# Running both layers' products as pairs of 64-row matmuls, with the order of issue taken from a list of operations

## The chip, the cores and the metric

One Trainium2 chip, one of its cores. The metric is device time in microseconds (us) of one execution, from three timed runs, and one further execution is recorded by the hardware profiler. Engines in the profile: PE is TensorE's matmul, PEld its weight load, DVE VectorE, ACT ScalarE, POOL GpSimd, SP SyncE, which here issues every DMA.

## What is computed

A softmax over 7 taps per position and head weighs a causal window of `x` (8192 positions of 192 features), and the result goes through two two-layer networks with 2048 hidden units each, one with a leaky ReLU, one with a squared ReLU. Weights are float64 and are split on the chip.

```python
w = softmax(weight_gen)                       # (2, 4096, 8 heads, 7 taps)
x = einsum('bshk,bskhg->bshg', w, window(x))  # 8192 x 192
h = x @ w_in;  x = maximum(0.01 * h, h) @ w_out         # 192 -> 2048 -> 192
h = x @ w_in2; r = maximum(h, 0); out = (r * r) @ w_out2
```

## The kernel before

Positions are worked on in 16 blocks of 512 (`tb`), hidden units in 16 chunks of 128 (`fc`). A phase is one network on one block, 16 steps; the phases run (0,0), (0,1), (1,0), (0,2), (1,1), (0,3) and so on, 32 in all, so 512 steps. Every float32 operand is held as a high and a low part in the type fp32r, and a product is high x high + low x high + high x low.

- `mm1` (L376) computes a chunk of hidden units: five matmuls with 128 x 128 weights on 512 columns. The 192 input features are 128 ("a") and 64 ("b"); the weights of the 64 lie twice in one tile, high in 64 rows and low in the other 64, and the moving tiles `bh`, `bl` hold the 64 features twice, so two matmuls cover them.
- `act_a` (L384, L385; L389, L390) applies the nonlinearity on ACT, `act_b` makes `gh` (L402, DVE, or ACT for the steps in `GH_SWAP`) and the low part `gl` (L404, DVE).
- `mm2` follows `LAG` = 3 steps behind. Network 0 (L417 to L421): five matmuls of 512 columns into `pa`, `pb`. Network 1 (L431, L434): the activations are the weights, `wo2` moves, four pairs of 384 and 192 columns into four banks `po`, whose rows are then positions, so the output needs no transposing.
- PSUM: two banks `ph`, two for `pa`, `pb`, four for `po`. Each network has accumulators of its own.
- `end1` turns the sums of network 0 into the input of network 1 with a DMA that swaps two halves (L446, L447); `end2` adds and stores.
- `conv_steps` is the windowed sum on DVE (softmax, 13 passes over 768 elements at L269 and L295), then a transposition: by PE for the first three blocks (`tr`), by DVE and a trip through DRAM for the others (`blocks`, `fr`).
- `Piece` turns 28 pieces of weights into high and low parts (ACT L138, L163; DVE L147 to L164); they are due in the first three phases.
- The order on each engine is the order of the main loop, with hand-set slots for the windowed sums (`CONV_AT`) and the pieces (`DUE`). All waits follow from the tiles.

Of the kernel before, what the change touches and what calls it, by code (L numbers as in the profile page):

```python
# [19 lines left out]
ORDER = [['b0', 'a0', 'o0', 'a1', 'o3', 'o1', 'o2', 'b1', 'a2', 'a3', 'o4', 'o5', 'o6', 'o7'], ['a0', 'o1', 'b0', 'o0', 'b1', 'a2', 'a1', 'o3', 'o2', 'a3', 'o4', 'o5', 'o7', 'o6']]  # L20
DUE = [[-2, -1, 1, 2, 3, 4, 5, 6, 7, 8, 9, 11, 12, 13], [18, 20, 22, 24, 28, 29, 30, 33, 36, 38, 39, 40, 44, 45]]
ENGINES = [[1, 1, 0]] * 28
POOL_TAPS = [3, 3, 3]
CONV_AT = [[0, 1, 4, 5, 6, 6, 7, 7, 8, 8, 10, 11, 12, 14, 14], [0, 0, 1, 4, 8, 8, 10, 13, 17, 18, 25, 26, 26, 28, 30]]
SIDE_AT = [[0, 1, 3, 4, 5, 6, 7, 8, 9, 10, 12, 14], [0, 1, 3, 4, 10, 11, 15, 17, 19, 20, 21, 22]]
GL_POOL = []
GH_SWAP = [0, 12, 14, 16, 17, 18, 22, 26, 31, 32, 33, 34, 35, 39, 40, 41, 44, 45, 47]
# [3 lines left out]
def kernel(  # L31
# [13 lines left out]

    nc = tc.nc
# [5 lines left out]
    G = D // H  # L52
# [3 lines left out]
    TPP = NT // P  # L56
    PPB = S // TPP
# [3 lines left out]
    NTB = TPP // TB  # L61
    NFC = FF // P
    DA = P
    DB = D - P
    CH = 4
    NCH = TPP // CH
    WCH = 4
    SW = FF // WCH
    OC = 2
    PH3 = 0  # L70
    PTAPS = dict(enumerate(POOL_TAPS))
    side_t = {}
# [26 lines left out]
    wo1 = {
        "ah": const.tile([P, NFC, DA], F32R, name="wo1ah"),  # L100
        "al": const.tile([P, NFC, DA], F32R, name="wo1al"),
        "b": const.tile([P, NFC, 2 * DB], F32R, name="wo1b"),
    }
    wo2 = const.tile([P, NFC, 2 * D], F32R, name="wo2")
# [5 lines left out]


    class Piece:
        def __init__(self, kind, l, c):
            self.kind, self.l, self.c = kind, l, c

        def load(self):
            kind, l, c = self.kind, self.l, self.c
            self.raw = raw = st.tile([P, SW, 2], I32, name="raw", tag="raw", bufs=3)
            if kind == "o":
                self.n = OC * D  # L120
                src = (w_out1, w_out2)[l]
                nc.sync.dma_start(
                    out=raw[:, : self.n, :].rearrange("p (f e) w -> p f e w", f=OC),
                    in_=src[c * OC * P : (c + 1) * OC * P].rearrange("(f p) e w -> p f e w", p=P),
                )
                return
            self.n = SW
            src = (w_in1, w_in2)[l]
            if kind == "a":
                nc.sync.dma_start(out=raw, in_=src[0:DA, c * SW : (c + 1) * SW, :])  # L130
            else:
                for h in range(2):
                    o = (2 * c + h) * SW
                    nc.sync.dma_start(out=raw[h * DB : (h + 1) * DB], in_=src[DA:D, o : o + SW, :])

        def scale(self):
            self.u = st.tile([P, SW], F32, name="wu", tag="wu", bufs=3)[:, : self.n]
            nc.scalar.activation(self.u, self.raw[:, : self.n, 1].bitcast(F32), AF.Copy, scale=2.0**-112)  # L138

        def join(self):  # L140
            u, n = self.u, self.n
            self.f = a = st.tile([P, SW], F32, name="wa", tag="wa", bufs=3)[:, :n]
            ui, ai = u.bitcast(I32), a.bitcast(I32)
            lo = self.raw[:, :n, 0].bitcast(U32)

            def rest():
                nc.vector.scalar_tensor_tensor(u, lo, 2.0**-52, u, op0=ALU.mult, op1=ALU.mult)  # L147
                (nc.gpsimd, nc.vector)[self.feng].tensor_tensor(a, a, u, op=ALU.add)  # L148

            return [  # L150
                lambda: nc.vector.tensor_scalar(
                    ai, ui, 3, 0x7FFFFFF8, op0=ALU.logical_shift_left, op1=ALU.bitwise_and
                ),
                lambda: nc.vector.scalar_tensor_tensor(ai, ui, SIGN, ai, op0=ALU.bitwise_and, op1=ALU.bitwise_or),  # L154
                lambda: nc.vector.tensor_scalar(ui, ai, SIGN_EXP, None, op0=ALU.bitwise_and),  # L155
                rest,
            ]

        def split(self):
            kind, l, c, f = self.kind, self.l, self.c, self.f  # L160

            def halves(h, lo, v):
                (nc.scalar.copy, nc.vector.tensor_copy)[self.heng](h, v)  # L163
                (nc.gpsimd, nc.vector)[self.leng].tensor_tensor(lo, v, h.bitcast(F32), op=ALU.subtract)  # L164

            if kind == "a":
                cs = slice(c * SW, (c + 1) * SW)
                halves(wi[l]["ah"][:, cs], wi[l]["al"][:, cs], f)
            elif kind == "b":
                h, lo = self.u.bitcast(F32R), f.bitcast(F32R)  # L170
                halves(h, lo, f)
                for j in range(2):
                    o = (2 * c + j) * SW
                    js = slice(j * DB, (j + 1) * DB)
                    nc.sync.dma_start(out=wi[l]["b"][0:DB, o : o + SW].bitcast(F32), in_=h[js].bitcast(F32))
                    nc.sync.dma_start(out=wi[l]["b"][DB:P, o : o + SW].bitcast(F32), in_=lo[js].bitcast(F32))
            else:
                fs = slice(c * OC, (c + 1) * OC)
                r = f.rearrange("p (f e) -> p f e", f=OC)
                if l == 0:  # L180
                    halves(wo1["ah"][:, fs, :], wo1["al"][:, fs, :], r[:, :, 0:DA])
                    halves(wo1["b"][:, fs, 0:DB], wo1["b"][:, fs, DB : 2 * DB], r[:, :, DA:D])
                else:
                    halves(wo2[:, fs, 0:D], wo2[:, fs, D : 2 * D], r)


    pieces = [
        (d, Piece(k[0], l, int(k[1:]))) for l in range(2) for d, k in zip(DUE[l], ORDER[l])
    ]
    for q, (d, p) in enumerate(pieces):  # L190
        p.feng, p.leng, p.heng = ENGINES[q]
    due = dict(pieces)


    x_flat = x.rearrange("b (p t) d -> (b p) t d", t=TPP)
    wg_flat = weight_gen.rearrange("b (p t) h k -> (b p) t h k", t=TPP)
    out_flat = out.rearrange("(p t) d -> p t d", t=TPP)
    xc_t = {}
    wg_t = {}
    wn_t = {}  # L200

    def load_chunk(c):
        xc = xp.tile([P, HALO + CH, D], F32, name="xc", tag="xc")
        wg = xp.tile([P, CH, H, K], F32, name="wg", tag="wg")
        if c == 0:
            nc.sync.dma_start(out=wg, in_=wg_flat[:, 0:CH])
            nc.gpsimd.memset(xc[0:1, 0:HALO, :], 0.0)
            nc.gpsimd.memset(xc[PPB : PPB + 1, 0:HALO, :], 0.0)
            nc.sync.dma_start(out=xc[:, HALO : HALO + TB, :], in_=x_flat[:, 0:TB, :])
            for b in range(B):  # L210
                o = TPP - HALO
                nc.sync.dma_start(
                    out=xc[b * PPB + 1 : (b + 1) * PPB, 0:HALO, :],
                    in_=x[b, o : o + (PPB - 1) * TPP, :].rearrange("(p t) d -> p t d", t=TPP)[:, 0:HALO, :],
                )
        else:
            nc.sync.dma_start(out=wg, in_=wg_flat[:, c * CH : (c + 1) * CH])
            nc.sync.dma_start(out=xc[:, HALO:, :], in_=x_flat[:, c * CH : (c + 1) * CH, :])
            nc.sync.dma_start(out=xc[:, 0:HALO, :], in_=xc_t[c - 1][:, CH : CH + HALO, :])
# [386 lines left out]
```

## Time and profile before

| | us |
|---|---|
| median of three runs (1262.72 to 1264.82) | 1264.58 |
| the profiled execution | 1262.62 |
| its span in the trace | 1260.8 |
| PE busy | 1207.7 (96%) |
| PE weight loads busy | 1023.9 (81%) |
| DVE busy | 822.7 (65%) |
| ACT busy | 678.0 (54%) |

Matmuls are pipelined, and their busy times overlap: a 512-column matmul shows 0.39 to 0.41 us of busy time, while one starts every 0.23 us. So a rate is read from the distance of starts, not from busy times. The same holds in smaller measure for ACT and DVE. The span is divided, in the reading below, into the time up to the first product, the first three phases, the 29 phases after them, and the end.

### The profile page before, as it was taken

The numbers are of one execution on the slowest core, as the hardware profiler recorded it, in microseconds if no ns is written. First come the engines' busy times: TensorE is split into PE (matmuls) and PEld (weight loads), VectorE is DVE, ScalarE is ACT, GpSimd is POOL, SyncE is SP. The second block draws the span as 40 slices with busy tenths as digits, with TensorE's granted clock in tenths as the row PEclk, the third lists the DMA queues.
The fourth block names the chain that finished last, engine by engine and source line by source line (L and its number), as shares of the span: only waits on it lengthen the run. The fifth ranks groups of instructions, "written<-read, shape, count | busy, mean of one in ns | idle before, by whom it ended". The sixth has DMA issues, their size and how long they took to land.

```text
span 1260.8 us, 16315 instructions
## 1 busy us (share of the span) xinstructions
PE 1207.7 (96%) x5912; PEld 1023.9 (81%) x5912; DVE 822.7 (65%) x1413; ACT 678.0 (54%) x1246; POOL 2.8 (0%) x8
## 2 busy tenths in 40 slices
PE   1689899999999999999999999999999999999997
PEld 1467688988888898888888888888888889888896
DVE  7999975757566575756657575665757556573453
ACT  2555665555555464555546455554555555455553
POOL 0000000000000000000000000000000000000000
PEclk9899999999999999999999999999999999999999
DMA  6424310202011020200202010020201100010000
GB/s 196 117 89 116 108 46 8 66 13 74 13 26 60 1 74 13 69 17 10 72 5 73 13 59 28 9 67 11 74 13 56 30 10 30 13 38 13 9 14 13
DMA packets 41120, 55.70 MB, mean 44 GB/s; under 512 B 4178, under 2 KB 30290, under 8 KB 41040
## 3 DMA queue, kind: packets, MB, share of 16 engines
q1 hardware_dynamic: 41040, 54.66, 14.4%
q8 instruction: 46, 0.75, 0.2%
q14 instruction: 34, 0.28, 0.1%
HBM read 28.11 MB, written 11.40 MB: 31 GB/s over the span
## 4 chain that ended last, share of the span: by engine, by line
PE 89%; DVE 8%; issue 1%; ACT 1%; DMA 0%; SPq 0%; DVEq 0%
PE ph L376 45%; PE po L431 15%; PE po L434 7%; PE pa L417 4%; PE pb L419 4%; PE pa L421 4%; PE pb L420 4%; PE pa L418 4%; DVE tmp L269 1%; DVE gl L404 1%; DVE wu L147 1%; DVE wa L154 1%; DVE wa L148 1%; DVE att L295 1%; DVE wu L155 1%
## 5 line engine op out<-in xcount | busy, mean ns | idle before, releaser
L404 DVE TENSOR_TENSOR gl<-g,gh 128x512 fp32r<-128x512 f32 x512 | 353.5, 691 | 260.9 <-ACT gh L385 232.9
L431 PE MATMUL po<-wo,gh 128*128 128x384 f32 x1024 | 307.1, 355 | 0.0
L384 ACT ACTIVATE g<-ph 128x512 f32<-128x512 f32 x256 | 153.5, 600 | 248.0 <-PE ph L376 246.8
L389 ACT ACTIVATE g<-ph 128x512 f32<-128x512 f32 x256 | 153.1, 598 | 198.7 <-PE ph L376 198.7
L434 PE MATMUL po<-wo,gl 128*128 128x192 f32 x1024 | 257.4, 251 | 2.5 <-DVE gl L404 2.5
L434 PEld LDWEIGHTS po<-wo,gl 128*128 128x128 f32 x1024 | 195.7, 191 | 14.1 <-DVE gl L404 3.2
L431 PEld LDWEIGHTS po<-wo,gh 128*128 128x128 f32 x1024 | 193.0, 188 | 11.9
L390 ACT ACTIVATE g<-g 128x512 f32<-128x512 f32 x256 | 162.1, 633 | 8.1
L402 DVE CAST gh<-g 128x512 fp32r<-128x512 f32 x247 | 104.1, 422 | 79.2 <-ACT g L390 79.2
L385 ACT ACTIVATE gh<-ph 128x512 fp32r<-128x512 f32 x256 | 152.3, 595 | 0.0
L376 PE MATMUL ph<-xah,wi0ah 128*128 128x512 f32 x256 | 103.7, 405 | 8.1 <-ACT wi0ah L163 4.5
L376 PE MATMUL ph<-xah,wi0al 128*128 128x512 f32 x256 | 102.9, 402 | 3.5 <-DVE wi0al L164 3.5
L376 PE MATMUL ph<-xah,wi1ah 128*128 128x512 f32 x256 | 105.2, 411 | 0.3 <-ACT gh L385 0.3
L417 PE MATMUL pa<-gh,wo1ah 128*128 128x512 f32 x256 | 102.5, 400 | 2.7 <-ACT wo1ah L163 2.2
L418 PE MATMUL pa<-gh,wo1al 128*128 128x512 f32 x256 | 102.2, 399 | 2.4 <-DVE wo1al L164 2.4
L420 PE MATMUL pb<-gl,wo1b 128*128 128x512 f32 x256 | 102.2, 399 | 2.3 <-DVE gl L404 2.3
L376 PE MATMUL ph<-xbl,wi0b 128*128 128x512 f32 x256 | 102.8, 402 | 0.0
L419 PE MATMUL pb<-gh,wo1b 128*128 128x512 f32 x256 | 102.4, 400 | 0.0
L421 PE MATMUL pa<-gl,wo1ah 128*128 128x512 f32 x256 | 102.3, 400 | 0.0
L376 PE MATMUL ph<-xbl,wi1b 128*128 128x512 f32 x256 | 102.1, 399 | 0.0
L376 PE MATMUL ph<-xbh,wi0b 128*128 128x512 f32 x256 | 102.1, 399 | 0.0
L376 PE MATMUL ph<-xal,wi0ah 128*128 128x512 f32 x256 | 101.8, 398 | 0.0
(79 smaller groups left out, 1564.9 us busy)
## 6 DMA issues: line engine op xcount, KB each, us to landing
xc<-xc SPq DMA_DIRECT2D x15, 576.0 KB
xc<-in_x_dram SPq DMA_DIRECT2D x16, 384.0 KB
raw<-in_moe_w_out_dram SPq DMA_DIRECT2D x16, 384.0 KB
sc<-xb SPq DMA_DIRECT2D x13, 384.0 KB
out_dram<-ot SPq DMA_DIRECT2D x52, 96.0 KB
raw<-in_moe_w_in_dram SPq DMA_DIRECT2D x8, 512.0 KB
bw<-bs SPq DMA_DIRECT2D x32, 128.0 KB
xa<-sc SPq DMA_DIRECT2D x52, 64.0 KB
```

Of the source, the lines that this page charges most:

```text
L376: nc.tensor.matmul(ph, lhsT=w[a][:, fs], rhs=xs[b], start=(i == 0), stop=(i == len(terms) - 1))
L384: nc.scalar.activation(g, ph, AF.Prelu, alpha=0.01)
L389: nc.scalar.activation(g, ph, AF.Relu)
L390: nc.scalar.activation(g, g, AF.Square)
L404: eng.tensor_tensor(gl, g, gh.bitcast(F32), op=ALU.subtract)
L417: nc.tensor.matmul(pa, lhsT=wo1["ah"][:, fc, :], rhs=gh, start=first, stop=False)
L418: nc.tensor.matmul(pa, lhsT=wo1["al"][:, fc, :], rhs=gh, start=False, stop=False)
L419: nc.tensor.matmul(pb, lhsT=wo1["b"][:, fc, :], rhs=gh, start=first, stop=False)
L420: nc.tensor.matmul(pb, lhsT=wo1["b"][:, fc, :], rhs=gl, start=False, stop=last)
L421: nc.tensor.matmul(pa, lhsT=wo1["ah"][:, fc, :], rhs=gl, start=False, stop=last)
L431: nc.tensor.matmul(po, lhsT=gh[:, ts], rhs=wo2[:, fc, :], start=first, stop=False, skip_group_check=True)
L434: nc.tensor.matmul(po[:, 0:D], lhsT=gl[:, ts], rhs=wo2[:, fc, 0:D], start=False, stop=last, skip_group_check=True)
```

## The change

- **Products.** The array is used as two halves of 64 rows, `HALVES`. A step is a pair of chunks. In `mm1` each half computes one chunk of the pair from three 64-feature blocks: "a", "b" and a new moving tile "s", "a" with its halves exchanged. That is nine pairs of 64-row matmuls for two chunks. In `mm2`, for both networks, the two halves take the upper and lower 64 rows of the same chunk, into accumulators of their own: ten pairs of 512 columns for two chunks. All matmuls now have 512 columns.
- **PSUM.** Two tiles `ph` of two banks; four banks `q0` to `q3` that both networks' accumulators use in turn.
- **Activations** are 1024 wide; network 1 takes three ACT passes (`Relu`, `Square` twice) and no DVE copy. `LAG` is 2 pairs.
- **Ends.** `total` adds the two halves' sums (one ACT copy, one DVE addition). `end2` transposes by DVE in 32 x 32 blocks and stores rows of 32 elements; positions are assigned to partitions so that these land right.
- **Inputs.** Windows are loaded whole; "s" comes from two DMAs (`swap`), for the first two blocks from a third PE transposition. Weight pieces are 18 instead of 28.
- **Order.** Every operation is entered in a list with an engine, an estimated cost and a priority; `Plan.issue` goes through the list once and issues, engine by engine, what can start first. PE keeps strict priority order.

```diff
-        terms = [("ah", "ah"), ("al", "ah"), ("b", "bh"), ("b", "bl"), ("ah", "al")]
-        for i, (a, b) in enumerate(terms):
-            nc.tensor.matmul(ph, lhsT=w[a][:, fs], rhs=xs[b], start=(i == 0), stop=(i == len(terms) - 1))
+            terms = [(wh, "h", s) for s in (0, 1, 2)] + [(wl, "h", s) for s in (0, 1, 2)]
+            terms += [(wh, "l", s) for s in (0, 1, 2)]
+            for i, (w, hl, s) in enumerate(terms):
+
+                for d in range(2):
+                    c = s if d == 0 else (1, 0, 2)[s]
+                    nc.tensor.matmul(
+                        ph.t[:, d, :],
+                        lhsT=w[HALVES[d], c, j, :],
+                        rhs=xs["asb"[s] + hl].t[HALVES[d]],
+                        start=(i == 0),
+                        stop=(i == len(terms) - 1),
+                    )
...
+        if l == 0:
+            pl.op("ACT", W, pr, [ph], [gh], lambda: nc.scalar.activation(gh.t, ph.t, AF.Prelu, alpha=0.01))
+            pl.op("ACT", W, pr, [ph], [g], lambda: nc.scalar.activation(g.t, ph.t, AF.Prelu, alpha=0.01))
+        else:
+            pl.op("ACT", W, pr, [ph], [g], lambda: nc.scalar.activation(g.t, ph.t, AF.Relu))
+            pl.op("ACT", W, pr, [g], [gh], lambda: nc.scalar.activation(gh.t, g.t, AF.Square))
+            pl.op("ACT", W, pr, [g], [g], lambda: nc.scalar.activation(g.t, g.t, AF.Square))
+        pl.op(
+            "DVE", dve(2 * N), pr + 0.7, [g, gh], [gl],
+            lambda: nc.vector.tensor_tensor(gl.t, g.t, gh.t.bitcast(F32), op=ALU.subtract),
+        )
...
+        if first:
+            acc_t[l] = [
+                [pl.buf(ps, [P, N], F32, n, f"q{2 * d + i}", 1) for i, n in enumerate(("pa", "pb"))] for d in range(2)
             ]
...
+        def prods(terms, g, begin, end):
+            for i, (c, w) in enumerate(terms):
+                for d in range(2):
+                    wt = wo[l][HALVES[d], 2 * j + c, :]
+                    nc.tensor.matmul(
+                        acc[d][w == "b"].t,
+                        lhsT=wt[:, {"ah": slice(0, P), "b": slice(P, 2 * P), "al": slice(2 * P, 3 * P)}[w]],
+                        rhs=g.t[HALVES[d], c, :],
...
+        for n, (ks, g) in enumerate(((("ah", "al"), gh), (("b",), gh), (("ah",), gl), (("b",), gl))):
...
+    def total(acc, i, v, hold, pr):
+        o = pl.op("ACT", act(N), pr, [acc[1][i]], [v, *hold], lambda: nc.scalar.copy(v.t, acc[1][i].t))
+        pl.op(
+            "DVE", dve(N), pr, [acc[0][i], v], [v],
+            lambda: nc.vector.tensor_tensor(v.t, acc[0][i].t, v.t, op=ALU.add),
+        )
...
+    def end2(tb, acc, pr):
+        oa, ob, bw = wide("oa"), wide("ob"), wide("bw")
+        total(acc, 0, oa, [], pr)
+        total(acc, 1, ob, [bw], pr)
+        ta = pl.buf(sb, [P, N], F32, "ta", "c", 3)
+        pl.op("SP", 0.5, pr, [ob], [bw], lambda: nc.sync.dma_start(out=bw.t[0:Q], in_=ob.t[Q:P]), late=0.5)
+        pl.op("DVE", dve(N), pr + 1, [oa], [ta], lambda: nc.vector.transpose(ta.t, oa.t))
...
+            for c in range(n):
+                v = src.t[32 * c : 32 * c + 32].rearrange("a (u e) -> a u e", e=32)
+                nc.sync.dma_start(out=out_rows[:, tb, :, 32 * (c0 + c) : 32 * (c0 + c + 1)], in_=v)
...
+        pl.op("SP", 2.0, pr + 1, [ta], [], lambda: store(ta, 0, 4), late=2.0)
+        pl.op(
+            "DVE", dve(N), pr + 2, [ob, bw], [ob],
+            lambda: nc.vector.tensor_tensor(ob.t[0:Q], ob.t[0:Q], bw.t[0:Q], op=ALU.add),
+        )
+        pl.op("DVE", dve(N), pr + 2, [ob], [oa], lambda: nc.vector.transpose(oa.t[0:Q], ob.t[0:Q]))
+        pl.op("SP", 1.0, pr + 2, [oa], [], lambda: store(oa, 4, 2), late=1.0)
...
+        local_sum(0, 0)
+        weights("i", 0, (1, 1, 2, 2, 2))
+        weights("o", 0, (1, 1, 2, 2, 2))
+        weights("i", 1, (2,) * 4)
+        weights("o", 1, (2,) * 4)
...
+                if j == (LAG if tb else 0) and l == 0 and tb + 1 < NTB:
+                    local_sum(tb + 1, at[0, tb + 1] - (4 if tb else 1), gate=() if tb == 0 else (starts[0, tb - 1],))
+                o = mm1(l, tb, j, i)
+                if j == 0:
+                    starts[l, tb] = o
+                activate(l, tb, j, i + 0.5)
             if i >= LAG:
-                mm2(*steps[i - LAG])
...
+                mm2(*steps[i - LAG], i + 0.5)
+        pl.issue()
```

## Rows read from the trace of the kernel before

**Rows 1.** The page's head and its part 4, shares of the last chain.
```profile
span 1260.8 us, 16315 instructions
...
PE 89%; DVE 8%; issue 1%; ACT 1%; DMA 0%; SPq 0%; DVEq 0%
```

**Rows 2.** Busy time by stretch; columns named in the first row, counts in brackets.
```profile
core 0: us, PE busy (x) PEld busy (x) DVE busy (x) ACT busy (x) POOL busy (x), PEclk, DMA share, GB/s
0.00:27.40 27.40, 1.96 (x9) 1.59 (x9) 20.36 (x33) 5.86 (x11) 2.81 (x8) 1.00 0.64 182
27.40:86.30 58.90, 44.83 (x153) 33.05 (x154) 57.19 (x116) 30.21 (x67) 0.00 (x0) 0.88 0.43 130
86.30:127.30 41.00, 39.06 (x162) 29.30 (x160) 38.65 (x71) 24.73 (x48) 0.00 (x0) 1.00 0.37 96
127.30:173.60 46.30, 42.00 (x208) 35.89 (x208) 44.84 (x84) 32.98 (x62) 0.00 (x0) 0.93 0.29 91
173.60:247.80 74.20, 74.20 (x370) 63.35 (x369) 46.72 (x79) 40.55 (x75) 0.00 (x0) 1.00 0.12 37
...
173.60:1253.40 1079.80, 1079.80 (x5386) 924.03 (x5384) 660.86 (x1111) 583.78 (x1060) 0.00 (x0) 1.00 0.11 32
```

**Rows 3.** Instructions of L376 from 128 to 250 us: count, durations, first and last start.
```profile
L376 PE MATMUL ph<-xah,wi0ah x17: 393/394/413, 173.6 to 247.8; 128*128 128x512 f32 x17
```

**Rows 4.** PE in order of time (start us, us), one step of network 0.
```profile
561.07 0.39 PE L376 MATMUL ph<-xah,wi0ah 128*128 128x512 f32 x1
...
563.40 0.39 PE L376 MATMUL ph<-xah,wi0ah 128*128 128x512 f32 x1
```

**Rows 5.** PE in order of time, one step of network 1.
```profile
602.89 0.41 PE L376 MATMUL ph<-xah,wi1ah 128*128 128x512 f32 x1
...
604.07 0.34 PE L431 MATMUL po<-wo,gh 128*128 128x384 f32 x1
...
605.20 0.41 PE L376 MATMUL ph<-xah,wi1ah 128*128 128x512 f32 x1
```

**Rows 6.** Weight loads (PEld) in order of time, around two short matmuls.
```profile
602.23 0.19 PEld L431 LDWEIGHTS po<-wo,gh 128*128 128x128 f32 x1
602.34 0.19 PEld L434 LDWEIGHTS po<-wo,gl 128*128 128x128 f32 x1
```

**Rows 7.** Groups by line: busy us, mean ns, idle before and releaser.
```profile
L404 DVE TENSOR_TENSOR gl<-g,gh 128x512 fp32r<-128x512 f32 x512 | 353.5, 691 | 260.9 <-ACT gh L385 232.9 <-PE po L434 1.4 <-PE ph L376 0.9
L402 DVE CAST gh<-g 128x512 fp32r<-128x512 f32 x247 | 104.1, 422 | 79.2 <-ACT g L390 79.2
...
L148 DVE TENSOR_TENSOR wa<-wa,wu 128x384 f32<-128x384 f32 (+1 forms) x28 | 17.2, 615 | 1.0
```

**Rows 8.** The last chain from 27 to 60 us: start us, us it takes.
```profile
36.37 0.60 DVE gl L404
...
54.28 0.87 DVE att L269
```

**Rows 9.** ACT in order of time: two 512-wide passes in a row.
```profile
93.42 0.59 ACT L445 COPY bs<-pb 128x512 f32<-128x512 f32 x1 [2.12 <-PE pb L420]
93.90 0.59 ACT L448 CAST xah<-pa 128x512 fp32r<-128x512 f32 x1
```

**Rows 10.** All engines at the end, in order of time.
```profile
1252.64 1.18 ACT L459 COPY ot<-po 128x192 f32<-128x192 f32 x4 [2.44 <-PE po L434]
...
1252.99 1.22 DVE L460 TENSOR_TENSOR ot<-po,ot 128x192 f32<-128x192 f32 x4 [1.54 <-ACT ot L459]
1253.02 0.36 PE L431 MATMUL po<-wo,gh 128*128 128x384 f32 x1
1253.21 0.25 PE L434 MATMUL po<-wo,gl 128*128 128x192 f32 x1
1253.38 2.44 SPq L463 DMA_DIRECT2D out_dram<-ot  x4
```

**Rows 11.** Waits of SP's queue: total us, times, longest.
```profile
SPq L334 <- DMA sc<-xb: 27.0, 13, 2.8
```

More of the change, by code (lines that the diff above doesn't have):

```diff
@@ L26, with __init__ @@
-GL_POOL = []
-GH_SWAP = [0, 12, 14, 16, 17, 18, 22, 26, 31, 32, 33, 34, 35, 39, 40, 41, 44, 45, 47]
+class Buf:
+    def __init__(self, make=None, ring=None):
+        self.make, self.ring = make, ring
+        self.writers, self.readers = [], []
+        self.left = 0
+        self.end = 0.0
+        self.t = None
+class Op:
+    def __init__(self, eng, cost, fn, prio, deps, bufs, late):
+        self.eng, self.cost, self.fn, self.prio = eng, cost, fn, prio
+        self.deps, self.bufs, self.late = deps, bufs, late
+        self.end = None
@@ new lines, with __init__, buf, op @@
+class Plan:
+    def __init__(self):
+        self.ops = []
+        self.rings = {}
+    def buf(self, pool, shape, dtype, name, tag, bufs):
+        return Buf(lambda i: pool.tile(shape, dtype, name=name, tag=f"{tag}_{i}", bufs=1), (tag, bufs))
+    def op(self, eng, cost, prio, reads, writes, fn, after=(), late=0.0):
+        deps = set(after)
+        for b in reads:
+            deps.update(b.writers)
+        for b in writes:
+            deps.update(b.readers or b.writers)
+        o = Op(eng, cost, fn, prio, deps, [], late)
+        for b in dict.fromkeys([*reads, *writes]):
+            o.bufs.append(b)
+            b.left += 1
+        for b in reads:
+            b.readers.append(o)
+        for b in writes:
+            if b.readers:
+                b.writers, b.readers = [], []
+            b.writers.append(o)
+        self.ops.append(o)
+        return o
+    def issue(self, gap=0.07):
+        free = {}
+        wire = 0.0
+        queues = {}
+        for o in self.ops:
+            queues.setdefault(o.eng, []).append(o)
+        for q in queues.values():
+            q.sort(key=lambda o: o.prio)
+        order = {}
+        def start_of(o):
+            t = 0.0
+            for d in o.deps:
+                if d.end is None:
+                    return None
+                t = max(t, d.end + (gap if d.eng != o.eng else 0.0))
+            need = {}
+            for b in o.bufs:
+                if b.t is None and b.make:
+                    need[b.ring] = need.get(b.ring, 0) + 1
+            for (tag, n), k in need.items():
+                slots = self.rings.setdefault(tag, [None] * n)
+                ends = sorted(s.end + gap if s else 0.0 for s in slots if not (s and s.left))
+                if len(ends) < k:
+                    return None
+                t = max(t, ends[k - 1])
+            return t
+        left = len(self.ops)
+        while left:
+            best = None
+            for e, q in queues.items():
+                f = free.get(e, 0.0)
+                pick = None
+                for n, o in enumerate(q):
+                    if e == "PE" and n:
+                        break
+                    if n > 60:
+                        break
+                    s = start_of(o)
+                    if s is None:
+                        continue
+                    s = max(s, f)
+                    if pick is None or s < pick[0] - 0.15:
+                        pick = (s, n, o)
+                    if s <= f:
+                        break
+                if pick and (best is None or pick[0] < best[0]):
+                    best = (*pick, e)
+            if best is None:
+                raise RuntimeError("no operation can start: " + str([(e, q[0].prio) for e, q in queues.items() if q]))
+            s, n, o, e = best
+            queues[e].pop(n)
+            for b in o.bufs:
+                if b.t is None and b.make:
+                    slots = self.rings[b.ring[0]]
+                    i = min((s.end if s else -1.0, i) for i, s in enumerate(slots) if not (s and s.left))[1]
+                    slots[i] = b
+                    b.t = b.make(i)
+            o.fn()
+            free[e] = s + o.cost
+            if o.late:
+                wire = max(wire, s + o.cost) + o.late
+                o.end = wire + 2.0
+            else:
+                o.end = s + o.cost
+            o.at = s
+            for b in o.bufs:
+                b.left -= 1
+                b.end = max(b.end, o.end)
+            left -= 1
@@ L104 @@
[L104 to L124, printed above, removed]
-                )
[L126 to L152, printed above, removed]
-                ),
-                lambda: nc.vector.scalar_tensor_tensor(ai, ui, SIGN, ai, op0=ALU.bitwise_and, op1=ALU.bitwise_or),
-                lambda: nc.vector.tensor_scalar(ui, ai, SIGN_EXP, None, op0=ALU.bitwise_and),
-                rest,
-            ]
[L159 to L184, printed above, removed]
@@ L187 @@
[L187 to L219, printed above, removed]
-        xc_t[c], wg_t[c] = xc, wg
@@ L458, in end2 @@
[L458 to L469 removed]
+    NPR = NFC // 2
@@ new lines, with act, dve @@
+    Q = 64
+    HALVES = (slice(0, Q), slice(Q, P))
+    LAG = 2
+    EARLY = 2
+    R = TB * H
+    const = ctx.enter_context(tc.tile_pool(name="const", bufs=1))
+    sb = ctx.enter_context(tc.tile_pool(name="sb", bufs=2))
+    dram = ctx.enter_context(tc.tile_pool(name="dram", bufs=2, space=bass.MemoryType.DRAM))
+    ps = ctx.enter_context(tc.tile_pool(name="ps", bufs=2, space=bass.MemoryType.PSUM))
+    pl = Plan()
+    def act(n):
+        return 0.17 + n / 1200
+    def dve(n):
+        return (n + 151) / 960
@@ new lines, with x_set, swap, go @@
+    XS = ("ah", "al", "sh", "sl", "bh", "bl")
+    def x_set():
+        return {k: pl.buf(sb, [P, N], F32R, f"x{k}", f"x{k}", 3) for k in XS}
+    x1 = []
+    taken = []
+    def swap(xs, pr):
+        for k in "hl":
+            def go(k=k):
+                to, of = xs["s" + k].t, xs["a" + k].t
+                nc.sync.dma_start(out=to[0:Q].bitcast(F32), in_=of[Q:P].bitcast(F32))
+                nc.sync.dma_start(out=to[Q:P].bitcast(F32), in_=of[0:Q].bitcast(F32))
+            pl.op("SP", 1.0, pr, [xs["a" + k]], [xs["s" + k]], go, late=1.0)
@@ new lines, in mm2 @@
+    def mm2(l, tb, j, pr):
+        gh, gl = g_t.pop((l, tb, j))
+        first, last = j == 0, j == NPR - 1
+        if first:
+            acc_t[l] = [
+                [pl.buf(ps, [P, N], F32, n, f"q{2 * d + i}", 1) for i, n in enumerate(("pa", "pb"))] for d in range(2)
+            ]
+        acc = acc_t[l]
+        def prods(terms, g, begin, end):
+            for i, (c, w) in enumerate(terms):
+                for d in range(2):
+                    wt = wo[l][HALVES[d], 2 * j + c, :]
[3 more added lines that the diff above has]
+                        rhs=g.t[HALVES[d], c, :],
+                        start=begin and i == 0,
+                        stop=end and i == len(terms) - 1,
+                    )
+        w = wo_b[l][j]
+        for n, (ks, g) in enumerate(((("ah", "al"), gh), (("b",), gh), (("ah",), gl), (("b",), gl))):
+            terms = [(c, k) for c in range(2) for k in ks]
+            to = [a[ks[0] == "b"] for a in acc]
+            pl.op(
+                "PE", len(terms) * MM, pr + 0.01 * n, [g, w], to,
+                lambda terms=terms, g=g, n=n: prods(terms, g, first and n < 2, last and n >= 2),
+            )
+        if last:
+            (end1, end2)[l](tb, acc, pr - 1)
@@ new lines, in total, with wide, end1, other @@
+    def total(acc, i, v, hold, pr):
+        o = pl.op("ACT", act(N), pr, [acc[1][i]], [v, *hold], lambda: nc.scalar.copy(v.t, acc[1][i].t))
+        pl.op(
+            "DVE", dve(N), pr, [acc[0][i], v], [v],
+            lambda: nc.vector.tensor_tensor(v.t, acc[0][i].t, v.t, op=ALU.add),
+        )
+        return o
+    def wide(name):
+        return pl.buf(sb, [P, N], F32, name, "w", 4)
+    def end1(tb, acc, pr):
+        xs = x_set()
+        x2.append(xs)
+        sa, bs, bw = wide("sa"), wide("bs"), wide("bw")
+        taken.append(total(acc, 0, sa, [*xs.values()], pr))
+        total(acc, 1, bs, [bw], pr)
+        def other():
+            nc.sync.dma_start(out=bw.t[0:Q], in_=bs.t[Q:P])
+            nc.sync.dma_start(out=bw.t[Q:P], in_=bs.t[0:Q])
+        pl.op("SP", 1.0, pr, [bs], [bw], other, late=1.0)
+        ah, al, bh, bl = (xs[k] for k in ("ah", "al", "bh", "bl"))
+        pl.op("ACT", act(N), pr + 1, [sa], [ah], lambda: nc.scalar.copy(ah.t, sa.t))
+        pl.op(
+            "DVE", dve(N), pr + 1, [sa, ah], [al],
+            lambda: nc.vector.tensor_tensor(al.t, sa.t, ah.t.bitcast(F32), op=ALU.subtract),
+        )
+        swap(xs, pr + 1)
+        pl.op(
+            "DVE", dve(N), pr + 2, [bs, bw], [bs], lambda: nc.vector.tensor_tensor(bs.t, bs.t, bw.t, op=ALU.add)
+        )
+        pl.op("ACT", act(N), pr + 2, [bs], [bh], lambda: nc.scalar.copy(bh.t, bs.t))
+        pl.op(
+            "DVE", dve(N), pr + 2, [bs, bh], [bl],
+            lambda: nc.vector.tensor_tensor(bl.t, bs.t, bh.t.bitcast(F32), op=ALU.subtract),
+        )
@@ L474, with weights, begin @@
     phases.append((1, NTB - 1))
-    PH3 = 0
-    if PH3:
-        phases = [(0, 0), (0, 1), (0, 2), (1, 0), (1, 1)]
-        for tb in range(3, NTB):
-            phases += [(0, tb), (1, tb - 1)]
-        phases.append((1, NTB - 1))
-    def plan(fs, tb):
-        if tb < 2 + PH3:
-            at = CONV_AT[tb]
-        else:
-            at = [0, 2, 3, 4, 6, 8, 10, 12, 14, 15, NFC + 1]
-            at += [NFC + 7 - k for k in range(len(fs) - 15, 0, -1)]
-            at += [NFC + 7, NFC + 7, NFC + 12, NFC + 14]
-        return list(zip(at, fs))
-    GH = set(GH_SWAP)
-    POOL_GL = set(GL_POOL)
-    steps = [(l, tb, fc) for l, tb in phases for fc in range(NFC)]
-    todo = []
-    with tc.manual_schedule():
-        load_chunk(0)
-        warm = cv.tile([P, 1], F32, name="warm", tag="warm", bufs=1)
+    at = {ph: i * NPR for i, ph in enumerate(phases)}
+    steps = [(l, tb, j) for l, tb in phases for j in range(NPR)]
+    def weights(kind, l, sizes):
+        j = 0
+        for n in sizes:
+            piece(kind, l, j, n, at[l, 0] + j + (LAG if kind == "o" else 0))
+            j += n
+    warm = const.tile([P, 1], F32, name="warm")
+    def begin():
         nc.vector.memset(warm, 0.0)
@@ L503 @@
         make_identity(nc, ident)
-        first = [p for d, p in pieces[:3]]
-        for p in first:
-            p.load()
-        load_chunk(1)
-        todo = conv_steps(0)
-        for f in todo[:4]:
-            f()
-        todo = todo[4:]
-        for _ in range(2):
-            todo.pop(0)()
-        side = side_t[0]
-        while side:
-            side.pop(0)()
-        first[0].scale()
-        first[1].scale()
-        for p in first[:2]:
-            for f in p.join():
-                f()
-                if todo[3:]:
-                    todo.pop(0)()
-            p.split()
@@ L579 @@
+    Plan.last = pl
 _INS = ["x", "weight_gen", "moe_w_in", "moe_w_out", "moe2_w_in", "moe2_w_out"]
```

526 lines of the change are left out of this document (226 added, 300 removed).

## The prediction

> **What bounds the kernel now.** I read the shares of the last chain first, then the busy time by stretch, then the starts on PE inside one step, then what surrounds the end. PE carries 89% of the last chain and DVE 8% [rows 1]. The stretches say where each counts [rows 2]. From 173.6 us, where the first step of phase (0,2) starts [rows 3], to 1253.4, PE is busy for the whole stretch at full clock, while DVE and ACT are busy for 61% and 54% of it: 29 phases in which only PE's rate counts. From 27.4 to 173.6 it is the other way: DVE is busy for 57.19 + 38.65 + 44.84 = 140.7 of 146.2 us (96%) and PE waits for weights that DVE is splitting; the granted clock there falls to a mean of 0.88 and 0.93 in two stretches, where PE had waited. So a change of PE's work pays in the 29 late phases, and a change of DVE's work in the first three.
>
> PE's rate has to be taken from starts. A step of network 0 lasts 563.40 - 561.07 = 2.33 us for ten matmuls of 512 columns, 0.233 each [rows 4]. A step of network 1 lasts 2.31: 1.18 for `mm1` and 1.13 for its four pairs of 384 and 192 columns, 0.283 a pair [rows 5]. The mean of both is 2.32, and 464 x 2.32 = 1076.5, plus the three lagging `mm2` (3 x 1.13), makes the 1079.8 of the stretch. The term is closed.
>
> **PE, late phases.** Let t be the distance from one pair of 64-row matmuls to the next. A step of the new kernel, two chunks of one network, has 9 + 10 = 19 pairs, so 19t against 2 x 2.32 = 4.64 us now. In columns: `mm1` goes from 5 to 4.5 matmuls per chunk, `mm2` of network 0 stays at 5, and that of network 1 rises from 4 x 576/512 = 4.5 to 5. The sum is 19.0 against 19.5, a gain of only 2.6%; the rest comes from network 1's four short pairs, which cost 1.13 us where 2304 columns at 0.233 per 512 would cost 1.05. Everything hangs on t, and no row of before shows a 64-row matmul. The bounds:
> - Below: weight loads. Two loads that followed each other as closely as any I found start 0.11 us apart [rows 6], and a pair needs two; if they share one path, t is no less than about 0.216.
> - Above: if the halves don't run together, t = 2 x 0.233 = 0.466.
> - Between: four PE instructions (two loads, two matmuls) were put through in 0.283 us in the short pairs [rows 5]; a pair at 0.233 asks for them 18% faster than any row shows for long.
>
> I take 0.233. It is the nearest row: a 512-column matmul whose weights load behind its predecessor, with two loads fitting into it. The halves touch different rows and different PSUM banks, so I see nothing that they would share but the path of instructions and that of loads. Then 232 steps x 19 x 0.233 = 1027.1, against 1076.5: 49.4 saved.
>
> **Sharing the accumulators.** `mm2` of the next phase wants `q0` to `q3` one `mm1` after the last `mm2` of this one, 9 x 0.233 = 2.1 us, and the "a" sums are complete 2 x 0.233 before that. Let T be the end of the step's `mm1`. "a" is complete at T + 1.88, visible some 0.17 later (a matmul's 0.39 of busy time less its 0.233 [rows 4]). ACT is in 1024-wide passes: two 512-wide ones start 0.48 apart [rows 9], so at most 0.96 for 1024. Two passes end at T + 2.1, the copy takes 0.59 [rows 9], the addition 0.69 (L404's, the same shape [rows 7]): T + 3.4 if DVE is free, T + 4.5 if it has just begun a 1024-wide subtraction. PE wants the banks at T + 2 x 2.21 = T + 4.4. So the wait is hidden unless DVE's order is unlucky; behind the addition on DVE stand `gl` and the windowed sum, which have a step of slack. Bounds 0 and 1 us for each of 29 boundaries; I take 0.15: 4.4 us.
>
> **ACT and DVE, late phases.** Per two phases (70.8 us) ACT has 8 x 2 + 8 x 3 passes x 0.96 = 38.4 plus about 4 for copies and casts, 60%. DVE: a 512-wide subtraction occupies 0.60 and a 768-wide pass 0.87 of the chain [rows 8], so 1.05 ns an element and 0.06 fixed, 1.14 for 1024; 16 x 1.14 + 13 x 0.87 + about 11 for the rest = 41, 57% (now 46.7 of 74.2 [rows 2]). The casts of L402, 247 on DVE [rows 7], are gone and cost ACT what is in the sum. Neither becomes a bound; if one did, the cover is 30 us per two phases. More DMA (the swaps, 32-element stores) has a share of 0.12 to grow from [rows 2], and each lands a phase or more before its use: nothing.
>
> **The first three phases.** DVE sets the pace up to step 24, so its work is the term. Pieces go from 28 [rows 7] to 18: 59 instructions fewer at 0.06 is 3.5, the columns stay. `gl`: 48 x 0.60 and seven casts at about 0.36 (0.422 [rows 7] less the 0.06) against 24 x 1.14, 3.9 less. The third transposed tile adds 2 x 0.60, the ends one pass and slightly longer ones, 0.8. Net 5.4 less: (0,2) starts at 168.2. PE alone would be there at 27.4 + 24 x 4.43 = 134, so DVE still decides. The first product: a third PE transposition (about 2 us) against a smaller first piece; I leave it at 27.4. For the list's order against the hand-set one I keep 15 us either way.
>
> **The end.** Now from PE's last slot (1253.21 + 0.09) to the span's end: 7.5 us, of which 5.0 follow SP's last issue (1253.38 + 2.44) [rows 10]. After: result visible 0.17, second ACT copy 0.59, addition 0.69, a DMA hop, addition, transposition (0.69 each), two issues of 0.6 (2.44 / 4) and the same 5.0. The hop I take from a wait for a DMA of the kind, 27.0 / 13 = 2.1 [rows 11], and 0.5 to issue. Sum 11.6.
>
> **Sum.** 168.2 + 1027.1 + 4.7 (two lagging `mm2`) + 4.4 + 11.6 = 1216.0 of span. The profiled execution of before took 1262.62 for a span of 1260.8, 1.8 outside it: 1217.8. The median of the runs is 2.0 above that execution: 1219.8, say 1220, 3.5% faster. The margin of 44.6 us is 0.010 us on each of 232 x 19 = 4408 pairs, so the change turns slower at t = 0.243.
>
> **The rivals.**
> - *The path of instructions decides (the other side).* PE needs four instructions a pair instead of two per full matmul. At 0.283, the densest that lasts in the trace, 4408 x 0.050 = 220 more: 1440. From t = 0.243 on it is slower than before; at 0.258, halfway, 1330. For it: no row shows 58 ns an instruction for long. Against it: what makes the short pairs dear fits their loads as well [rows 6]. By the Trainium skill, "TensorE: Matmul & The Clock Gate", section "Wait — 56ns, not 53.3ns?", a sequencer without hardware decode spends about 62 ns per MATMUL; if a load cost it as much, four would make 0.248 and some 1286 us, an estimate from that page; no row here shows it.
> - *The halves overlap only in part.* If a half's load must follow its partner's matmul start and the next pair waits for the later half, a load slot of 0.11 is added to each pair: t = 0.34, 4408 x 0.107 = 472 and some 15 in the first phases: about 1705. For it: no row of before shows that a half can run ahead of the other. Against: that order alone delays one half by a slot once, not each time. The Trainium skill's page named above, section "Measured speedup vs the span model", has four row tiles at 3.07 times one; that share, 0.77, would make t = 0.303 and about 1528 us, an estimate from the page. Its page "TensorEngine Tiling (Array Packing)", section "Key Properties", has tiles load and multiply in parallel, which is what I forecast.
> - *The halves don't run together, so the change doesn't do what it says.* t = 0.466: 4408 x 0.233 = 1027 more, and the first phases then take 27.4 + 24 x 19 x 0.466 = 240 instead of 168: about 2320.
> - *Boundaries wait.* The list puts a third ACT pass, two casts and a 1024-wide subtraction ahead of copy and addition: 0.96 + 0.96 + 1.14 on T + 3.4 is T + 6.4, 2 us late, 29 x 1.85 = 54 more: 1274. It turns slower at 1.7 us each.
> - *Pairs go faster.* If the 0.020 over 512 / 2400 = 0.213 is a change of weights that one half hides for the other, t falls to the loads' 0.216: 75 less, 1145.
>
> **How the numbers follow.** Forecast 0.58, with t from 0.230 to 0.240, boundaries from 0 to 0.6 and the first phases 15 either way: 1190 to 1255. Instructions 0.18, of which 0.07 below 1290; partial overlap and none together 0.06; boundaries 0.10 (1225 to 1290), half of it faster; faster pairs 0.08. To hold eight in ten the range takes the forecast, the boundaries and the lower part of the instructions' case: 1185 to 1290. A measurement of this kernel tells about 0.2% from no change. Faster: 0.58 + 0.08 + 0.05 = 0.71; same 0.02; slower 0.27.
>
> **What would show it.** In a late phase: starts of pairs 0.233 apart with both halves starting close together (right), or starts of single matmuls that far apart (no overlap). First `mm2` of a phase waiting for DVE's addition: more than 0.3 us means the boundary is priced too low. The first product of (0,2) at 153 to 183. If DVE's share is over 90% in late phases, I have missed work.

## The result and the profile after

The changed kernel takes 1281.4 us (median of four executions, 1279.5 to 1283.7) against 1264.5: a ratio of 1.0138, 95% interval 1.0118 to 1.0157, so 1.4% slower, more than its interval leaves to noise. 1220 was forecast.

| span in the trace, us | before | forecast | after |
|---|---|---|---|
| to the first product | 27.4 | 27.4 | 39.3 |
| the first three phases | 146.2 | 140.8 | 185.9 |
| from (0,2) to PE's last slot | 1079.7 | 1036.2 | 1047.8 |
| the end | 7.5 | 11.6 | 8.9 |
| whole span | 1260.8 | 1216.0 | 1281.9 |

The gain in the late phases is there: 31.9 us. The first two rows lose 51.6.

The page's head, the busiest engines and the shares of the last chain (now 80% PE, 8% DMA, where DMA had 0% [rows 1]):

```profile
span 1281.9 us, 22668 instructions
PE 1172.7 (91%) x9752; PEld 936.2 (73%) x9752; DVE 741.9 (58%) x887; ACT 745.7 (58%) x826; POOL 0.7 (0%) x6
...
PE 80%; DVE 9%; DMA 8%; ACT 1%; issue 1%; SPq 1%; DVEq 0%; ACTq 0%
```

Busy time by stretch, to be set beside [rows 2]: the first three phases, (0,2) and (1,1), (0,3) and (1,2), then all from (0,3) to the end of the products.

```profile
core 0: us, PE busy (x) PEld busy (x) DVE busy (x) ACT busy (x) POOL busy (x), PEclk, DMA share, GB/s
39.30:225.20 185.90, 127.20 (x885) 99.47 (x887) 141.70 (x195) 86.99 (x105) 0.00 (x0) 0.83 0.39 97
225.20:304.90 79.70, 74.12 (x612) 59.19 (x610) 53.60 (x64) 45.90 (x51) 0.00 (x0) 0.96 0.28 74
304.90:376.30 71.40, 71.40 (x612) 57.48 (x610) 41.61 (x48) 44.72 (x50) 0.00 (x0) 1.00 0.23 56
304.90:1272.80 967.90, 967.90 (x8250) 775.19 (x8246) 524.06 (x596) 606.59 (x661) 0.00 (x0) 1.00 0.20 48
```

From 304.9 us on PE is busy without a gap at full clock, and two phases take 71.4 us where they took 74.2. In the first three phases DVE has 141.7 us of work where it had 140.7, but in 185.9 us instead of 146.2: 44 us idle instead of 5.5. PE waits with it, and its granted clock falls to a mean of 0.83 there.

PE in order of time, a late step; a row holds the two halves of one or more pairs:

```profile
416.46 0.40 PE L492 MATMUL ph<-xah,wi1h 64*128 64x512 f32 x2
...
418.57 1.10 PE L534 MATMUL pa<-gh,wo 64*128 64x512 f32 x8
...
420.91 0.40 PE L492 MATMUL ph<-xah,wi1h 64*128 64x512 f32 x2
```

Nine pairs in 2.11 us and ten in 2.34: t = 0.234, where [rows 4] had 0.233 for one full matmul. The halves run together; in the records of single matmuls from 305 us on the second starts 3 or 4 ns after the first in 99% of the pairs.

What waits in the first three phases: the five longest pieces of the chain of work that ends last, up to 225.2 us (start us, us), then waits of the engines, then of SP's queue (total us, times, longest).

```profile
4.38 18.40 DMA xc<-in_x_dram
41.61 17.56 DMA raw<-in_moe_w_out_dram
116.80 15.97 DMA raw<-in_moe_w_in_dram
182.11 21.35 DMA xc<-in_x_dram
203.47 5.86 DMA bw<-bs
```

```profile
DVE att L407 <- DMA xc<-in_x_dram: 20.5, 2, 14.5
ACT wu L261 <- DMA raw<-in_moe_w_in_dram: 33.8, 4, 20.9
```

```profile
SPq L240 <- DMA xc<-in_x_dram: 14.9, 1, 14.9
SPq L574 <- DMA xc<-in_x_dram: 11.6, 1, 11.6
```

Four of the five pieces are DMAs of 16 to 21 us. Each either is a window load (`xc`) or shares the DMA engines with one: the piece at 41.61 was issued 7 us behind the load of block 1's window, that at 116.80 some 8 us behind block 2's. And SP issues in order: twice it stood for 15 and 12 us with other DMAs behind it until a window had landed. In the records its DMAs take eight semaphores in strict turn (all 491 here), and one whose semaphore still belongs to a DMA that has not landed waits for it; so one slow load stops the queue. In the kernel before, the longest DMA on this chain is the first window, of much the same size (951 KB in its DMAs, 948 here):

```profile
2.11 5.84 DMA xc<-in_x_dram
```

Why a window takes so long shows in the DMA share, the mean busy share of 16 engines, of stretches in which hardly anything else moves:

```profile
8.00:20.00 12.00, 0.00 (x0) 0.00 (x0) 0.41 (x2) 0.00 (x0) 0.00 (x0) 1.00 0.13 32
198.00:201.00 3.00, 3.00 (x30) 2.40 (x28) 0.00 (x0) 1.44 (x2) 0.00 (x0) 1.00 0.25 69
365.00:371.00 6.00, 6.00 (x54) 4.83 (x52) 1.46 (x2) 4.45 (x5) 0.00 (x0) 1.00 0.25 73
```

0.13 is two of 16 DMA engines, 0.25 is four. By the kernel's `window`, the load at 8 us has a source of [2][32][1920] elements (2 groups of 32 rows), the later ones [4][32][1920]. What was issued with it waits behind it: the first window's smaller loads, of 15 and 32 rows, end only at 20.8 to 22.0 us.

### The profile page after: what moved, and what is told of

Read it like the earlier page. It is cut to its first block, busy times and chain, and to the rows that moved or that the text cites. A ratio compares the mean times of both kernels' runs of the same rounds, so it can differ in the third digit from the quotient of the medians.

```text
span 1281.9 us, 22668 instructions
## 1 busy us (share of the span) xinstructions
PE 1172.7 (91%) x9752; PEld 936.2 (73%) x9752; DVE 741.9 (58%) x887; ACT 745.7 (58%) x826; POOL 0.7 (0%) x6
## 4 chain that ended last, share of the span: by engine, by line
PE 80%; DVE 9%; DMA 8%; ACT 1%; issue 1%; SPq 1%; DVEq 0%; ACTq 0%
PE ph L492 37%; PE pa L534 26%; PE pb L534 17%; DMA xc<-in_x_dram 4%; DVE tmp L407 2%; DMA raw<-in_moe_w_in_dram 2%; DVE att L415 1%; DMA raw<-in_moe_w_out_dram 1%; DVE gl L517 1%; DVE wu L281 1%; DVE wa L271 1%; DMA bw<-bs 0%; DVE wa L287 0%; DVE wu L277 0%; DVE wa L265 0%
## 5 line engine op out<-in xcount | busy, mean ns | idle before, releaser
L517 DVE TENSOR_TENSOR gl<-g,gh 128x1024 fp32r<-128x1024 f32 x256 | 313.0, 1223 | 408.4 <-ACT g L514 270.8
L534 PE MATMUL pa<-gh,wo 64*128 64x512 f32 x2048 | 286.7, 398 | 16.1 <-DVE sa L558 14.5
L509 ACT ACTIVATE gh<-ph 128x1024 fp32r<-128x1024 f32 x128 | 131.6, 1028 | 260.7 <-PE ph L492 260.7
L534 PEld LDWEIGHTS pa<-gh,wo 64*128 64x128 f32 x2048 | 194.6, 187 | 67.8 <-DVE sa L558 16.1
L512 ACT ACTIVATE g<-ph 128x1024 f32<-128x1024 f32 x128 | 131.4, 1027 | 147.4 <-PE ph L492 147.4
L534 PE MATMUL pa<-gl,wo 64*128 64x512 f32 x1024 | 164.5, 399 | 11.0 <-DVE gl L517 10.9
L534 PE MATMUL pb<-gh,wo 64*128 64x512 f32 x1024 | 163.6, 397 | 2.1 <-DVE bs L558 2.1
L534 PE MATMUL pb<-gl,wo 64*128 64x512 f32 x1024 | 163.9, 398 | 0.0
L514 ACT ACTIVATE g<-g 128x1024 f32<-128x1024 f32 x128 | 135.9, 1062 | 3.5
L513 ACT ACTIVATE gh<-g 128x1024 fp32r<-128x1024 f32 x128 | 135.8, 1061 | 3.6
L510 ACT ACTIVATE g<-ph 128x1024 f32<-128x1024 f32 x128 | 130.6, 1020 | 0.5 <-DVE gl L517 0.5
L492 PE MATMUL ph<-xah,wi0h 64*128 64x512 f32 x256 | 53.0, 409 | 28.3 <-ACT wi0h L299 25.7
```

The source lines that it names most:

```text
L492: nc.tensor.matmul(ph.t[:, d, :], lhsT=w[HALVES[d], c, j, :], rhs=xs["asb"[s] + hl].t[HALVES[d]], start=(i == 0), stop=(i == len(terms) - 1),)
L509: pl.op("ACT", W, pr, [ph], [gh], lambda: nc.scalar.activation(gh.t, ph.t, AF.Prelu, alpha=0.01))
L510: pl.op("ACT", W, pr, [ph], [g], lambda: nc.scalar.activation(g.t, ph.t, AF.Prelu, alpha=0.01))
L512: pl.op("ACT", W, pr, [ph], [g], lambda: nc.scalar.activation(g.t, ph.t, AF.Relu))
L513: pl.op("ACT", W, pr, [g], [gh], lambda: nc.scalar.activation(gh.t, g.t, AF.Square))
L514: pl.op("ACT", W, pr, [g], [g], lambda: nc.scalar.activation(g.t, g.t, AF.Square))
```

## The experiments

e1 to e3 are made from the changed kernel, e4 and e5 from e1, e6 from e4, e7 from e6; "..." in a diff stands for edits left out, which the expectations name. "(0,2)" is the start of that phase in the profiled execution; 225.2 in the changed kernel and 173.6 in the kernel before.

| kernel | first product | (0,2) | median us | ratio to before |
|---|---|---|---|---|
| changed | 39.3 | 225.2 | 1281.4 | 1.0138 (1.0118 to 1.0157) |
| e1_one_block_a_load | 27.6 | 183.8 | 1235.0 | 0.9773 (0.9741 to 0.9805) |
| e2_half_columns | 34.5 | 208.8 | 1263.5, one run | |
| e3_two_windows | 44.0 | 217.6 | 1268.3, one run | |
| e4_three_raw | 27.4 | 182.7 | 1236.4 | 0.9766 (0.9742 to 0.9789) |
| e5_small_pieces | 27.2 | 191.2 | 1244.1 | 0.9831 (0.9804 to 0.9857) |
| e6_three_raw_wg4 | 26.7 | 180.9 | 1233.2 | 0.9744 (0.9720 to 0.9768) |
| e7_gl_first | 26.5 | 183.2 | 1235.2 | 0.9764 (0.9734 to 0.9794) |

**e1_one_block_a_load: the outer dimension of the window load.**

```diff
-                nc.sync.dma_start(out=xv(), in_=window(0, BI, 0, A, tb, 0, HALO + TB))
+                for i in range(BI):
+                    nc.sync.dma_start(out=xv()[i * A : (i + 1) * A], in_=window(i, 1, 0, A, tb, 0, HALO + TB))
...
-            nc.sync.dma_start(out=xv()[2 * A : P], in_=window(2, 2, 0, A, 0, 0, HALO + TB))
+            for i in range(2, BI):
+                nc.sync.dma_start(out=xv()[i * A : (i + 1) * A], in_=window(i, 1, 0, A, 0, 0, HALO + TB))
```

> The window of x is loaded with one DMA for each of the four groups of 32 partitions instead of one DMA for all four (two for the first block). Theory A: a load whose outer dimension is 4 (2 for block 0) is carried by that many of the 16 DMA engines, 32 pieces of 7680 bytes one after the other on each, so it takes 16 to 21 us; and since SP's DMAs take turns on nine semaphores, later DMAs queue behind it. Then each load lands in under 6 us, DVE's waits for xc (28 us) go below 6 us, (0,2) starts at 175 to 190 instead of 225, and the whole takes 1225 to 1245. Theory B, the single window buffer or the order of the list is the cause whatever a load takes: loads are shorter but (0,2) starts after 205 and the whole takes over 1260.

1235.0 us: the same bytes in the same pieces, and 46 us are back. The stretches of the first two windows' transfer and the first three phases:

```profile
2.60:7.90 5.30, 0.00 (x0) 0.00 (x0) 0.98 (x3) 0.39 (x1) 0.00 (x0) 1.00 0.96 182
24.20:31.70 7.50, 6.44 (x28) 4.64 (x28) 7.22 (x16) 2.69 (x5) 0.00 (x0) 1.00 0.98 192
...
27.60:183.80 156.20, 120.30 (x884) 92.39 (x886) 143.29 (x197) 88.51 (x106) 0.00 (x0) 0.86 0.43 112
```

The DMA engines are now busy to 0.96 and 0.98, with what moves beside the window; its pieces are over in 5 to 8 us. Of the 28.3 us that DVE waited for windows over the whole trace 0.5 are left by that name, and 2.1 at the first window that the profile puts down to a load of weights, which the waiting pass doesn't read. DVE's idle time in the three phases is 12.9 us instead of 44. The transfer under 6 us was expected for each window; the later ones took up to 7.7, beside other loads. Theory B, which had (0,2) after 205, falls. The nine semaphores of the expectation are eight in the records.

The Trainium skill has this rule, "DMA: Bandwidth & Descriptors", section "Why a DMA increments its semaphore by 16 and not by 1": a DMA issued from SP runs on the largest number of engines, up to 16, that divides the slowest dimension other than 1 of both access patterns. The traces agree for 2 (share 0.13), 4 (0.25) and 32 (0.96 and 0.98, other loads beside it).

**e2_half_columns: long pieces, or the outer dimension?** Two DMAs of half the columns, each still with 2 or 4 outside.

```diff
-                nc.sync.dma_start(out=xv(), in_=window(0, BI, 0, A, tb, 0, HALO + TB))
+                for r in (0, 5):
+                    nc.sync.dma_start(out=xv()[:, r * D : (r + 5) * D], in_=window(0, BI, 0, A, tb, r, r + 5))
...
```

> The window is loaded by two DMAs of half the columns each (3840 bytes a row), each still with an outer dimension of 4 (2 for block 0). Theory A, the outer dimension sets how many engines carry it: the same engines carry both, the second half lands 16 us or later after the issue as the whole did, time 1275 to 1290. Rival, long pieces of 7680 bytes are what is slow, or one DMA alone is: both halves land in 8 us or so, time under 1260.

1263.5 us, between the two theories' times. A stretch of block 0's load with nothing else moving:

```profile
8.00:12.50 4.50, 0.00 (x0) 0.00 (x0) 0.00 (x0) 0.00 (x0) 0.00 (x0) 1.00 0.13 49
```

The share is still 0.13. In the records of single DMA pieces 2.0 are in flight on average during block 0's load and 3.8 to 4.0 during the later ones; the changed kernel has 2.0 and 3.6 to 4.0. Two DMAs get no more engines than one. So the outer dimension holds, and its forecast of the time was wrong for another reason: two engines carry 49 GB/s instead of 32, since a piece of 3840 bytes takes 0.16 us there where one of 7680 takes 0.49. Block 0's load shrinks from 16.5 to 11.5 us, later ones from 12 to 18 down to 11 to 15. Why a long piece takes more time per byte stays open; few engines are not needed for it, as pieces of 7680 bytes take 0.55 to 0.60 us in e1.

**e3_two_windows: the single buffer.**

```diff
-        xc = pl.buf(sb, [P, HALO + TB, D], F32, "xc", "xc", 1)
+        xc = pl.buf(sb, [P, HALO + TB, D], F32, "xc", "xc", 2)
...
```

> Window loads as they are, but two window buffers instead of one (room is made by two instead of three buffers in the rings c and gh, which may cost some us in the late phases). Theory A: the first load and the queue behind each load stay slow, only the wait for the second and third window goes: (0,2) starts at 195 to 215. Theory B, the single buffer: (0,2) starts before 180.

(0,2) at 217.6, later even than theory A's 195 to 215. DVE waits for a window once, 10.3 us, but the second window's load is issued early and now stands in front of the first weights:

```profile
ACT wu L261 <- DMA raw<-in_moe_w_in_dram: 31.8, 1, 31.8
```

The first product moves to 44.0. Starting a slow transfer earlier lets it hold up the weights more. Still, the one run is 13 us faster than the changed kernel, and phase (1,1) takes 35.6 us again instead of 44.1: the single buffer is a smaller part of the loss, and the slow transfer the larger.

**e4_three_raw and e5_small_pieces: is the rest the landing of weights?** e1 is still 15.6 us later at (0,2) than forecast.

```diff
-        raw = pl.buf(sb, [P, SW, 2], I32, "raw", "raw", 2)
+        raw = pl.buf(sb, [P, SW, 2], I32, "raw", "raw", 3)
...
```

> As e1_one_block_a_load, with three instead of two buffers for raw weights (room is made by two instead of three buffers in the rings c and gh; the late phases of e3 showed this to cost under 0.1 us a phase). In e1 phase (0,2) starts at 183.8, 10 us later than in the kernel before and 15 later than forecast. Theory A: with two buffers a piece's load is only issued when the last-but-one piece has been used, and ACT and DVE wait for the landing (13.5 us of waits of ACT for raw in e1): (0,2) at 170 to 178, time 1222 to 1230. Theory B: the order on DVE fixed by the list (the windowed sum of block 1 ahead of the subtractions that PE waits for) is the rest: (0,2) after 181, time 1232 to 1238.

```diff
-    SW = 2 * 3 * P
+    SW = 3 * P
...
-        weights("i", 0, (1, 1, 2, 2, 2))
+        weights("i", 0, (1,) * 8)
...
```

> As e1_one_block_a_load, with 32 pieces of weights of one pair each instead of 18, and four raw buffers of half the size. Theory A (landing of the raw weights): more pieces in flight, (0,2) at 170 to 180, less some 14 x 6 x 0.06 = 5 us for more DVE instructions, so 1225 to 1233. Theory B (order or DVE's work): (0,2) at 188 or later, time over 1236.

Neither helps: (0,2) at 182.7 and 191.2. The buffers that e4 takes from two other rings cost it little: (0,2) and (1,1) together last 1.4 us longer than in e1. In e5 DVE has 148.0 us of work in the three phases for 273 instructions, against 143.3 for 197 in e1, so 0.06 us for each instruction more: that price of the forecast holds. Theory A falls. The stretch of e5, then, in e4, PE's longest waits after the first product, which are for `gl`:

```profile
27.20:191.20 164.00, 122.63 (x884) 93.09 (x886) 148.02 (x273) 90.27 (x131) 0.00 (x0) 0.88 0.38 102
...
PE pa L536 <- DVE gl L519: 17.3, 3, 11.0
```

**e6_three_raw_wg4: the small load of the same form.** The softmax weights, also [4][32] outside, by four DMAs.

```diff
+            for i in range(BI):
+                nc.sync.dma_start(out=to[i * A : (i + 1) * A], in_=wg_flat[i, :, tb])
...
```

> As e4_three_raw, with the softmax weights' load split by groups of 32 partitions like the window's. Its first landing is 5.8 us into the span and 3.0 in the kernel before. If it too is carried by four engines only, it lands by 4.5 and the first product starts 1 to 3 us earlier than in e4; if x is what DVE waits for, nothing changes (same within 1 us).

The first product starts 0.7 us earlier than in e4, inside the 1 us that the expectation gives to no change, and the whole is 1233.2, the fastest of all: 2.6% faster than the kernel before. DVE's first wait for these weights falls from 4.3 (e1) to 2.0, but it then waits longer for x (3.5 instead of 2.1). The difference to e4 is within what their intervals leave open.

**e7_gl_first: the order on DVE.**

```diff
-            "DVE", dve(2 * N), pr + 0.7, [g, gh], [gl],
+            "DVE", dve(2 * N), pr - 3.0, [g, gh], [gl],
...
```

> As e6_three_raw_wg4, with one number changed: in the list the subtraction gl, which PE waits for, stands ahead of the weight pieces and the windowed sums on DVE (priority step - 2.5 instead of step + 1.2). In e6 PE waits 18.6 us for gl in the first three phases, and DVE is busy for 142.0 of 154.3 us there. Theory B, the order is what is left: PE's waits for gl fall under 6 us, (0,2) starts 3 to 8 us earlier than 180.9, time 1225 to 1230. Rival: DVE's work is the bound and the order only moves the wait from gl to weights or windows: (0,2) at 179 to 183, time 1231 to 1235.

PE no longer waits for `gl` at all, but (0,2) starts at 183.2 and the time is 1235.2, which is the rival's case, just past its upper edge. The stretch of the three phases, and where the waits went, to what now stands behind:

```profile
26.60:183.10 156.50, 123.12 (x884) 94.58 (x886) 141.47 (x195) 87.24 (x104) 0.00 (x0) 0.85 0.38 107
...
PE pt L448 <- DVE att L422: 29.0, 2, 22.4
PE ph L499 <- DVE wi0l L304: 7.4, 3, 3.4
PE pb L541 <- DVE bs L565: 6.9, 2, 4.8
```

With the windows mended, DVE's work takes most of the first three phases again (141.5 of 156.5 us here), and this change of its order only moved what PE waits for. The 15 us in which DVE is idle are not explained by it.

## Why the prediction was wrong

The span missed by 65.9 us: 11.9 at the first product, 45.1 in the first three phases, 11.6 from there to PE's last slot, -2.7 at the end.

- **t = 0.233: right**, at 0.234. The three rivals on t (instructions, partial overlap, no overlap) fall, and the faster pairs too: 0.216 was not reached. The time of 1281 lies near the instruction rival's 1286 and the boundary rival's 1274, which is chance: in the late phases, where both were priced, neither mechanism occurs.
- **Shared accumulators: right in size in the late phases.** 0.15 us a boundary was taken. These phases take 35.61 and 35.76 us in turn, against 8 x 19 x 0.234 = 35.6. The only wait of PE's loads from 305 to 1270 us is this row:

```profile
PEld pa L534 <- DVE oa L558: 4.2, 13, 0.3
```

In the first three phases PE does wait for the sums that free a shared bank (`sa`, `bs`): 12.1 us after, 9.7 in e1. DVE makes these sums and has work for most of the time there; what the waits cost is not shown.

- **ACT and DVE in late phases: right**, 63% and 54% against 60% and 57%.
- **The late stretch** is 11.6 us over. 8.5 of these are one phase, (1,1), which takes 44.1 instead of 35.6: block 4's window, issued at 246, holds DVE until 262.5, with `gl` and the sums that PE waits for behind it. In e1 this phase takes 35.6.
- **"More DMA ... each lands a phase or more before its use: nothing" and "I leave it at 27.4": wrong, the step that failed.** The prediction names the swaps and the stores as new DMA and has no term for the window's new load, which it so takes for as quick as the 5.84 us load that it replaces. Its access pattern had changed from 128 rows to groups of 2 or 4 outside, and that set its speed: e1 only splits the load by these groups and takes 46 us off the median, while e2, with more DMAs of the old form, gets no more engines. Late, a load of 12 to 15 us does land in time; the same load in the first phases is on the path and delays what is queued with it. A mean DMA share hides this: it is 0.39 in the first three phases after, and was 0.37 before for the same stretch.
- **First three phases, "DVE sets the pace": right in the main from e1 on (143.3 of 156.2 us), not for the change as it stood**, where DVE was idle for 44 us. The 5.4 us less work on DVE did not come: 161.1 us of busy time from the start to (0,2) before, 160.9 after. The trace tells why, with each DVE instruction up to (0,2) counted until the next one starts: the pieces fall from 81.3 to 77.5 us and `gl` with its casts from 31.7 to 26.3, a little more than forecast. But the softmax rises from 5.8 to 8.1, since the list does it for four blocks before (0,2) and not for three, the windowed sums with a transposition from 34.2 to 37.5, two rises that the sum left out, and splits and ends from 8.4 to 12.1, where 2.0 more was allowed. With e1, the 15.6 us that are left against the forecast at (0,2) are 0.2 at the first product, 8.0 of DVE's work, and 12.9 of idle time where 5.5 had been assumed. Buffers (e4), smaller pieces (e5) and order (e7) did not take the idle time away, and its cause stays open.
- **The end**: 2.7 us shorter than priced, nearly all of it in one term: 2.5 us follow SP's last issue, which this row ends at 1279.37, where the 5.0 of the kernel before was taken.

```profile
1278.52 0.85 SPq L604 DMA_DIRECT2D out_dram<-oa  x2
```

The sign was forecast wrong. The rivals looked for the loss where the change was largest, on PE and at its boundaries, and none was about how a load is laid out. With that load mended the forecast of 1220 is 1.2% from e1's 1235.

## What to carry to other kernels

When a change lays data out anew, read the access pattern of each new DMA, not only its bytes: the outermost dimension decided here between 2, 4 and all of the 16 DMA engines, a factor of two to three in the transfer's time; halving the pieces helped less. A slow transfer that is hidden in the steady part can sit on the path at the start, so price it there by itself, with the transfers issued behind it on the same queue. And when a stretch loses time while its busiest engine has no more work than before, look at what that engine waited for before changing its order or buffers.

## What the runs showed that was not expected

Pieces of 7680 bytes ran at 32 GB/s on two DMA engines and pieces of 3840 bytes at 49. Two DMAs issued one behind the other with four groups outside had no more pieces in flight than one, about four. One slow load stopped SP's whole queue when its semaphore came round again. And 64-row pairs with their own weights each kept the distance of a single full matmul, 0.234 us, at four PE instructions in that time, denser than any row of the kernel before.
